# Which engine regroups q and k in front of the DMA transposes: VectorE or GpSimd

## The chip, the cores and the metric

The kernel runs on one core of a Trainium2 chip. The metric is the device time of one execution in microseconds (us); a shorter time is better. A core has engines with an instruction stream each: TensorE (PE in the profile; PEld is its weight loads), VectorE (DVE), ScalarE (ACT), GpSimd (POOL) and SyncE (SP). DMA transfers are issued from a queue of one of these engines; in this kernel from GpSimd's and SyncE's.

## The reference

Attention with a squared ReLU in place of the softmax, over 8 batches of 12 heads, 448 positions and 64 elements a head, and then a gated feed-forward layer over all 3584 tokens:

```python
scores = scale * np.matmul(q, k.transpose(0, 1, 3, 2))
attn = np.maximum(scores, 0.0) ** 2 / S
attn_out = np.matmul(attn, v)
x = attn_out.transpose(0, 2, 1, 3).reshape(B * S, H * D)      # 3584 x 768
gate = np.maximum(x @ w_gate, 0.0)                            # 768 x 1536
val = x @ w_val
return gate * val @ w_out                                     # 1536 x 768
```

Inputs and output are float32.

## The kernel before

The kernel works in 48 slots, one for each batch b (0 to 7) and each pair of heads hp (0 to 5). In a slot TensorE makes the scores of the pair (tile `sc_ps`), ScalarE takes their ReLU (`relu_part`, line 179), VectorE squares it from SBUF into SBUF (`square_part`, line 183, output `attn`), and TensorE multiplies by v (`av`, tile `xT_ps`), which VectorE copies out (line 213). The feed-forward layer of batch b-1 is cut into units and fed into the slots of batch b by `gap()`: `gv_unit` makes a gate product `g_ps` and a value product `v_ps`, of which ScalarE (line 236) and VectorE (line 241, output `hT`) make one operand of the last product; `out_unit` makes that last product (`o_ps`), and sends the rows out through SyncE's queue (line 265). `g_ps`, `v_ps` and `o_ps` share two PSUM buffers, so that a `v_ps` can begin only when the `v_ps` before it has been read by line 241.

The scores need q and k with the head's 64 elements on the partitions, that is transposed. Batches 0 and 1 are transposed on TensorE (`transposes`, line 172, copied out by VectorE in line 174). Batches 2 to 7 take another way, `dma_transposes(b)`, which is called once for each of them, in slot hp = 2 of the batch before: k (tile `kn`) is regrouped into `kr` by one copy of 128 partitions x 3072 bf16 elements (line 140), and four DMA transposes on SyncE's queue (line 143) take `kr` to `kT`; the same follows for q (`qn`, `qr`, `qT`). There is one `kr` and one `qr`, two each of `kn`, `qn`, `kT`, `qT` and v's tiles (`vn`, `vp`). In slot hp = 4 `key_pads` copies the last 64 keys out of `kT` (line 149, VectorE).

All loads are issued from GpSimd's queue (`dma_in`, line 91). `load_qk(b + 1)` and `load_v(b + 1)` stand in slot hp = 0 of batch b. Each instruction is kept in program order on its own engine (`pin`), and engines wait for one another only for data and for free buffers, so GpSimd's queue runs ahead of the others: it stops where a buffer isn't free. `load_v(b + 1)` overwrites the v tiles of batch b - 1, and so waits for the last `av` of batch b - 1. `load_qk(b + 2)`, which is next in that queue, overwrites the `kn` and `qn` of batch b, whose regrouping took place in batch b - 1, and so finds its buffers free as soon as its turn comes.

Of the kernel before, what the change touches and what calls it, by code (L numbers as in the profile page):

```python
# [16 lines left out]
def kernel(  # L17
# [14 lines left out]
    nc = tc.nc  # L32
# [25 lines left out]
    def pin(ins):  # L58
        return tc.keep_in_program_order(ins)
# [75 lines left out]
    def dma_transposes(b):  # L135

        n = b % NB
        for nat, grp, tr in ((kn_b[n], kr, kT_b[n]), (qn_b[n], qr, qT_b[n])):
            o = grp.rearrange("p i (h d) -> p i h d", d=D)
            pin(nc.vector.tensor_copy(o, nat.rearrange("p h i d -> p i h d")))  # L140
            for i in range(4):
                r = 128 if i < 3 else 64
                pin(nc.sync.dma_start_transpose(out=tr[:, :, i * 128:i * 128 + r], in_=grp[0:r, i, :]))  # L143
# [167 lines left out]
    for n, (b, hp) in enumerate(slots):  # L311
# [6 lines left out]
        if b == 0:  # L318
            relu2(*todo[0])
            if hp < HP - 1:  # L320
                kq_next = operands(b, hp + 1)
            relu2(*todo[1])
            relu2(*todo[2])
            scores_last(kq, attn)
            if prev:
                av(*prev)
            prev = this
            if hp == HP - 1:
                av(*prev)
        else:  # L330
            relu2(*todo[0])
            relu2(*todo[1])
            late.append(todo[2])
            gap()
            scores_last(kq, attn)
            if n + 1 < len(slots):
                kq_next = operands(*slots[n + 1])
            gap()
            av(*this)
            if b + 1 >= PE_B and b + 1 < B:  # L340
                if hp == 2:
                    dma_transposes(b + 1)
                if hp == 4:
                    key_pads(b + 1)
            if b > 1:
                gap()
# [46 lines left out]
```

## Time and profile before

| what | value |
|---|---|
| median of 3 runs | 446.57 us (446.33 to 449.02) |
| the profiled execution | 449.76 us, with a span of 447.7 us from the first to the last instruction |
| TensorE (PE) busy | 426.9 us, 95% of the span |
| VectorE (DVE) busy | 215.2 us, 48% |
| ScalarE (ACT) busy | 220.2 us, 49% |
| GpSimd (POOL) busy | 61.5 us, 14%, nearly all of it the issue of DMAs |
| line 140, both copies | 12 instructions, 11.4 us of VectorE |
| TensorE clock granted | 0.994 on average |

The profiled execution is one run with its own time: 2.06 us of it lie outside the span, and it is 3.2 us above the median of the three runs. Busy times are sums over an engine. TensorE has 20.8 us without work in the whole span, 8 us of them in the first 15 us. Where the batches begin on TensorE, by the first scores made from `kT` and `qT`: batch 2 at 90.5 us, batch 3 at 145.5 us, batch 6 at 297.5 us.

### The profile page before, as it was taken

What the parts mean: (1) busy time and instruction counts of PE and PEld (TensorE: products, weight loads), DVE (VectorE), ACT (ScalarE), POOL (GpSimd) and SP (SyncE); (2) the same over time, 40 slices, a digit from 0 to 9 for tenths busy, and PEclk for the clock granted to TensorE, in tenths of its full rate; (3) what the DMA queues carried; (4) which work ended last, traced back from release to release, by engine and by line L of the source; (5) the groups of instructions that cost most, each with busy time, mean ns of one, the idle gap of its engine ahead of it and who ended that gap; (6) DMA issues with size and microseconds to landing.
All of it is one profiled execution on the core that took longest, in us unless ns stands there. A gap on an engine that the chain in (4) does not pass through costs nothing.

```text
span 447.7 us, 10641 instructions
## 1 busy us (share of the span) xinstructions
PE 426.9 (95%) x4608; PEld 251.4 (56%) x4608; DVE 215.2 (48%) x382; ACT 220.2 (49%) x345; POOL 61.5 (14%) x89
## 2 busy tenths in 40 slices
PE   3879998899999999999999999999999999999995
PEld 1337554545566555665566555565556655666663
DVE  4682566535643556444653457455644445422210
ACT  3572565546454654654464565464455456442221
POOL 9624410430003100050001300020000000000000
PEclk9999999989999999999999999999999999999999
DMA  7999999997443914398153932471042200030014
GB/s 83 181 204 191 202 205 178 151 243 99 45 115 77 204 16 98 63 147 110 39 87 91 191 50 63 98 111 24 19 108 72 72 2 0 5 90 15 1 37 107
DMA packets 91887, 43.55 MB, mean 97 GB/s; under 512 B 66753, under 2 KB 88257, under 8 KB 91841
## 3 DMA queue, kind: packets, MB, share of 16 engines
q0 software_dynamic: 53568, 23.60, 42.6%
q1 hardware_dynamic: 38272, 19.28, 20.1%
q8 instruction: 36, 0.59, 0.5%
q14 instruction: 11, 0.08, 0.1%
HBM read 47.19 MB, written 11.01 MB: 130 GB/s over the span
## 4 chain that ended last, share of the span: by engine, by line
PE 79%; DMA 15%; POOL 2%; SPq 1%; DVE 1%; issue 1%; ACT 0%; POOLq 0%; DVEq 0%
PE g_ps L62 22%; PE o_ps L62 22%; PE v_ps L62 21%; PE sc_ps L62 7%; PE xT_ps L62 6%; DMA qn<-in_q_dram 5%; DMA kn<-in_k_dram 4%; DMA wv<-in_moe_w_val_dram 2%; DMA qT<-qr 2%; DMA vn<-in_v_dram 2%; SPq L143 1%; DVE attn L183 1%; POOL qn L91 1%; POOL wg L91 1%; POOL kn L91 1%
## 5 line engine op out<-in xcount | busy, mean ns | idle before, releaser
L179 ACT ACTIVATE r_sb<-sc_ps 128x896 bf16<-128x896 f32 x192 | 149.5, 826 | 43.7 <-PE sc_ps L62 43.7
L183 DVE TENSOR_TENSOR attn<-r_sb 128x896 bf16<-128x896 bf16 x192 | 104.8, 564 | 75.3 <-ACT r_sb L179 75.3
L62 PE MATMUL g_ps<-xT,wg 128*64 128x448 bf16 x1152 | 126.9, 356 | 0.2 <-DVE xT L213 0.2
L62 PE MATMUL v_ps<-xT,wv 128*64 128x448 bf16 x1152 | 125.7, 354 | 0.0
L62 PE MATMUL o_ps<-wo,hT 128*64 128x384 bf16 x1344 | 117.2, 327 | 0.0
L241 DVE TENSOR_TENSOR hT<-v_ps,g_sb 128x448 bf16<-128x448 f32 x96 | 60.0, 625 | 104.7 <-PE v_ps L62 104.7
L236 ACT ACTIVATE g_sb<-g_ps 128x448 bf16<-128x448 f32 x96 | 52.3, 545 | 106.8 <-PE g_ps L62 106.8
L62 PEld LDWEIGHTS <-hT 128*64 128x64 bf16 x1344 | 74.8, 110 | 38.1 <-issue 5.6
L62 PEld LDWEIGHTS <-wg 128*64 128x64 bf16 x1152 | 63.9, 110 | 48.9 <-issue 11.2
L62 PEld LDWEIGHTS <-wv 128*64 128x64 bf16 x1152 | 66.6, 110 | 43.3 <-issue 1.0
L262 ACT ACTIVATE o_sb<-o_ps 128x384 f32<-128x384 f32 x56 | 27.8, 496 | 72.1 <-PE o_ps L62 72.1
L213 DVE CAST xT<-xT_ps 128x448 bf16<-128x448 f32 x48 | 29.9, 624 | 23.6 <-PE xT_ps L62 22.0
L62 PE MATMUL xT_ps<-attn,vn 128*64 128x448 bf16 x288 | 37.3, 362 | 2.6 <-DVE attn L183 1.6
L91 POOL DMA_DIRECT2D vn<-in_v_dram x16 | 12.1, 765 | 191.0 <-PE xT_ps L62 186.0
L62 PE MATMUL sc_ps<-qT,kT 64*128 64x448 bf16 x216 | 26.7, 352 | 2.8 <-DMA qT<-qr 2.8
L62 PEld LDWEIGHTS <-vn 128*64 128x64 bf16 x288 | 17.0, 112 | 14.0 <-issue 3.8
L62 PE MATMUL sc_ps<-kq_sb 64*128 64x448 bf16 (+1 forms) x96 | 16.1, 417 | 2.3 <-DVE kq_sb L174 1.3
L62 PEld LDWEIGHTS <-kT 64*128 64x128 bf16 x216 | 7.6, 94 | 18.3 <-issue 15.0
L62 PE MATMUL xT_ps<-attn,vp 128*64 128x448 bf16 x96 | 17.7, 362 | 0.0
L91 POOL DMA_DIRECT2D kn<-in_k_dram x20 | 14.8, 768 | 13.6 <-PE kq_ps L172 12.7
L91 POOL DMA_DIRECT2D qn<-in_q_dram x20 | 14.7, 760 | 7.4 <-DMA qn<-in_q_dram 3.9
L91 POOL DMA_DIRECT2D vp<-in_v_dram x16 | 10.8, 692 | 17.1 <-PE g_ps L62 5.3
(27 smaller groups left out, 85.8 us busy)
## 6 DMA issues: line engine op xcount, KB each, us to landing
out_dram<-o_sb SPq DMA_DIRECT2D x56, 192.0 KB, 2.7
vn<-in_v_dram POOLq DMA_DIRECT2D x16, 288.0 KB, 7.2
kn<-in_k_dram POOLq DMA_DIRECT2D x7, 384.0 KB, 9.2
qn<-in_q_dram POOLq DMA_DIRECT2D x7, 384.0 KB, 11.2
wo<-in_moe_w_out_dram POOLq DMA_DIRECT2D x2, 1152.0 KB, 17.7
kn<-in_k_dram POOLq DMA_DIRECT2D x7, 288.0 KB, 10.0
qn<-in_q_dram POOLq DMA_DIRECT2D x7, 288.0 KB, 12.4
wg<-in_moe_w_gate_dram POOLq DMA_DIRECT2D x4, 384.0 KB, 9.5
```

Of the source, the lines that this page charges most:

```text
L62: pin(nc.tensor.matmul(o, lhsT=l, rhs=r, start=start, stop=stop, skip_group_check=True))
L91: pin(nc.gpsimd.dma_start(out=o, in_=i))
L143: pin(nc.sync.dma_start_transpose(out=tr[:, :, i * 128:i * 128 + r], in_=grp[0:r, i, :]))
L179: pin(nc.scalar.activation(r, src, AF.Relu))
L183: pin(nc.vector.tensor_tensor(dst, r, r, ALU.mult))
L213: pin(nc.vector.tensor_copy(xT[:, hp, :], ps))
L236: pin(nc.scalar.activation(g_sb, g_ps, AF.Relu))
L241: pin(nc.vector.tensor_tensor(hT[:, mf, col:col + S], v_ps, g_sb, ALU.mult))
L262: pin(nc.scalar.activation(out=o_sb[:, m], in_=o_ps, func=AF.Copy, scale=float(out_scale)))
```

## The change

The two regrouping copies of `dma_transposes` are issued on GpSimd instead of VectorE. Their operands, the DMA transposes behind them and every other line are the same. Since GpSimd's queue also holds the loads, the copies for batch b + 1 now stand in it behind `load_v(b + 1)` and ahead of `load_qk(b + 2)`.

```diff
         for nat, grp, tr in ((kn_b[n], kr, kT_b[n]), (qn_b[n], qr, qT_b[n])):
             o = grp.rearrange("p i (h d) -> p i h d", d=D)
-            pin(nc.vector.tensor_copy(o, nat.rearrange("p h i d -> p i h d")))
+            pin(nc.gpsimd.tensor_copy(o, nat.rearrange("p h i d -> p i h d")))
             for i in range(4):
                 r = 128 if i < 3 else 64
                 pin(nc.sync.dma_start_transpose(out=tr[:, :, i * 128:i * 128 + r], in_=grp[0:r, i, :]))
```

## The prediction

> **What bounds the kernel now.** I read the page's busy times and chain first, then the timelines of VectorE and TensorE around the copies, then GpSimd's own.
>
> ```profile
> PE 426.9 (95%) x4608; PEld 251.4 (56%) x4608; DVE 215.2 (48%) x382; ACT 220.2 (49%) x345; POOL 61.5 (14%) x89
> ...
> PE 79%; DMA 15%; POOL 2%; SPq 1%; DVE 1%; issue 1%; ACT 0%; POOLq 0%; DVEq 0%
> ```
>
> TensorE bounds it. Taking work off VectorE, which is half idle, brings nothing by itself. A copy counts only where TensorE waits, and the list of waits has two such places: 2.8 us for `qT` (once) and 1.6 us for squares (four times).
>
> ```profile
> 68.85 0.96 DVE L140 COPY kr<-kn 128x3072 bf16<-128x3072 bf16 x1 [0.43 <-DMA kn<-in_k_dram]
> ...
> 72.39 0.96 DVE L140 COPY qr<-qn 128x3072 bf16<-128x3072 bf16 x1 [2.58 <-DMA qn<-in_q_dram]
> ...
> 73.27 1.99 DVE L183 TENSOR_TENSOR attn<-r_sb 128x896 bf16<-128x896 bf16 x4
> ...
> 73.94 0.38 PE L62 MATMUL xT_ps<-attn,vn 128*64 128x448 bf16 x2 [0.86 <-DVE attn L183]
> ...
> 90.51 0.74 PE L62 MATMUL sc_ps<-qT,kT 64*128 64x448 bf16 x6 [2.83 <-DMA qT<-qr]
> ...
> 91.19 2.45 PE L62 MATMUL g_ps<-xT,wg 128*64 128x448 bf16 x12
> ...
> 93.43 1.89 PE L62 MATMUL v_ps<-xT,wv 128*64 128x448 bf16 x12
> ```
>
> (Timelines: start, length, engine; in brackets the idle time before and its releaser.) Both places belong to the first pair of copies, for batch 2. VectorE sits 2.58 us in front of a copy whose q hasn't landed, four squares queue behind it, and TensorE loses 0.86 us, and 0.15 and 0.16 behind that: 1.2 us. Then it waits 2.83 us for `qT`, and the next products run at a granted clock of 0.57 (91 to 95 us, by the windows): 2.45 and 1.89 us instead of 1.30 each, 1.7 us lost. The other five pairs cost TensorE nothing: the second, at 116.21 and 117.08, sits between a cast and a product of line 241 that was due at about 117.7, and no wait of TensorE follows.
>
> **What the change removes.** 12 copies of 0.95 us, 11.4 us of VectorE; on TensorE at most the 1.2 us, and these lie ahead of the wait for `qT`, which would take them back if `qT` lands when it does.
>
> **What it adds: the copy on GpSimd.** The trace has no such copy. Lowest: VectorE's own 0.95 us. Highest: GpSimd's only elementwise row with an input, the 128x128 affine_select, 349 ns; less the 100 ns of its one-element memsets that is 1.95 ns an element, so 3072 x 1.95 + 100 = 6.1 us. Between them lies ScalarE's ReLU, 896 elements in 826 ns: 3072 x 826 / 896 = 2.83 us. A copy does less for each element than a select with its comparison, and I know no reason for VectorE's rate on an engine of another kind: I take 2.83 us, and call it D. The Trainium skill (GPSIMD Engine Reference, 3.1 Elementwise) gives 1.03 cycles an element at 1.2 GHz for simple bodies, an estimate of 2.64 us; by it the sum below would be some 1.5 us less.
>
> **What moves.** Once GpSimd's queue holds the copies, they no longer stand in slot hp = 2 but run as soon as the queue reaches them, at the batch's start:
>
> ```profile
> 143.21 1.33 POOL L91 DMA_DIRECT2D vp<-in_v_dram  x2
> 144.51 1.54 POOL L91 DMA_DIRECT2D kn<-in_k_dram  x2
> ...
> 195.84 1.55 POOL L91 DMA_DIRECT2D kn<-in_k_dram  x2
> ```
>
> In place of these `kn` issues come the copies, at 144.5, 195.8, 247.2 and 298.6 us; their data landed 40 us before. Behind them on GpSimd wait only the loads of the batch after next, 2 x 2.83 = 5.7 us late: issued by about 153 and needed by the next copy at 195.8, with 10 to 13 us to landing. No cost; it would cost from about 30 us. The 48 transposes stay on SyncE behind the same output DMAs, and now run at the start of the batch instead of slot 2, beside loads; outputs come next at 185, so they hold up nobody, and `kT` is needed at the next batch's start. DMAs are the same in number and size. The third batch's pair runs when `kn` and `qn` land, at about 91.7 and 94.6 us (issues at 80.30 and 81.77, landing after 11.4 and 12.8).
>
> **Whether VectorE can run beside it.** No row has a VectorE instruction beside a GpSimd instruction that reads SBUF. Bounds: no delay, or every square waits for the copy's end. For no delay speaks that the square at 146.90 takes its usual 0.63 us beside an issue of GpSimd; but an issue reads no tile. For a delay speaks that VectorE's rates go with where its operands lie (copy from SBUF 3.2 elements a ns, square 1.6, cast from PSUM 0.7), so access to SBUF is what it spends its time on, and the copies now add another reader. I take the full wait. The Trainium skill (SBUF — State Buffer, Who interferes with whom) speaks against this change outright: a VectorE instruction with two SBUF inputs and a GpSimd instruction that reads SBUF share a port, and whichever comes second waits for the whole of the first; no trace here shows it yet. By that rule the squares wait and the products of line 241, with one input in PSUM, wait only behind them; without it the sum is that of the first rival.
>
> **The price at the start of a batch.** In the timeline before:
>
> ```profile
> 146.90 0.63 DVE L183 TENSOR_TENSOR attn<-r_sb 128x896 bf16<-128x896 bf16 x1 [4.58 <-ACT r_sb L179]
> ...
> 147.71 0.63 DVE L183 TENSOR_TENSOR attn<-r_sb 128x896 bf16<-128x896 bf16 x1 [0.18 <-ACT r_sb L179]
> ...
> 148.69 0.62 DVE L241 TENSOR_TENSOR hT<-v_ps,g_sb 128x448 bf16<-128x448 f32 x1 [0.36 <-PE v_ps L62]
> ...
> 149.23 0.92 DVE L183 TENSOR_TENSOR attn<-r_sb 128x896 bf16<-128x896 bf16 x2
> ...
> 149.75 1.30 PE L62 MATMUL v_ps<-xT,wv 128*64 128x448 bf16 x12
> ```
>
> If copy and square alternate: first copy from 144.51 to 144.51 + D, a square (0.55), second copy D, another square (0.45 to the next start), and only then line 241, due at 148.69. It is 2D + 1.0 - 4.18 = 2.5 us late; 0.44 us of slack remain before the `v_ps` at 149.75, so TensorE stands 2.0 us. If two squares slip in between the copies, line 241 is on time, and the squares of 149.23 end 2.0 us late, of which `av` at 150.88 absorbs about 1.1: 0.9 us. Middle 1.5. The batches at 195.84 and 298.6 reach their first square only 0.4 us behind the copy (196.28), and line 241 at 198.08: 2D + 1.0 - 2.24 - 0.44 = 4.0 us, or 2.7 by the other order; middle 3.4. The pair for batch 3 (from 91.7) by the same reckoning 0.7 to 2.1, say 1.0. A stand of 2.83 us was followed by the 1.7 us of low clock above; of the two longer ones I count one.
>
> The first pair: `kr` is ready 1.9 us later (D - 0.95). By the windows the DMA engines move loads at about 190 GB/s until 74 us, and the first `kT` transposes land only after 6.6 us, so part of this is hidden; `qT` lands at 90.4 plus 0 to 1.9 us. TensorE's 1.2 us are given back here by the wait. I take +1.0.
>
> Sum: 1.0 + 1.0 + 2 x 1.5 + 2 x 3.4 + 1.7 = 13.5 us on the span of 447.7, so 461.2; with the 2.06 around it 463.3, against 449.76. The runs' median is 3.2 us below the profiled one: 446.57 + 13.5 = 460.
>
> **Rivals.** (1) No delay of VectorE: the copies lie beside it, and only the first pair counts, 0 to 1.9 us: 447 to 448; at D = 6.1 it would be up to 5 us, 452. For it: nothing in the rows shows the opposite. Against: only the argument on SBUF access. (2) The wait holds and the copy is long. Each of the four starts grows by 2 us for each us of D in the alternating order: from D = 2.83 to 6.1 this adds 4 x 6.5 = 26 us, with low clock at all four (5 us more), the pair for batch 3 and the first another 10: 460 + 41 = about 500. For it: the affine_select row; against: the simpler work. (3) Faster. VectorE is no longer held 2.58 us by the q that hasn't landed, and the transposes, issued 1.9 us later, fall behind the backlog of loads and meet no competition, so that `qT` lands before TensorE, 1.2 us earlier, asks for it at 86.5: then 1.2 + 2.83 + 1.7 = 5.7 us go, 440.9. It decides only if `qT` lands 4 us earlier than now; against it stands that the next loads of `kn` and `qn`, issued at 79.41 to 82.5, share the DMA engines with the last `qT` transpose (issued 81.95, landed 8.4 us later), and would meet it later still.
>
> **How the numbers follow.** Forecast 0.50; rival 1 0.32 (0.05 of it slower by over 1%, with a long copy); rival 2 0.13; rival 3 0.05. One per cent, 4.5 us, is about what a measurement of this kernel tells from no change. Faster 0.05, same 0.27, slower 0.50 + 0.05 + 0.13 = 0.68. The range goes from 446 (rival 1's lower end with a little spread) to 480, which the full wait gives at D of about 4.2 (8 x 1.4 = 11 from the four starts, the clock 5, the other pairs 4); left out are most of rival 2 and rival 3. For the forecast alone it is 452 to 472.
>
> **What would show it.** The copies at POOL line 140 at the batch's start, of 2.8 us; squares of line 183 beside them of 2 to 3 us or with a gap in front of them; a wait of `v_ps` or `xT_ps` on VectorE of 1 to 4 us at 150, 200, 251 and 303 us; transposes about 20 us earlier. If squares beside the copies stay at 0.56 to 0.63 us without gaps, the forecast is wrong and rival 1 holds; a copy over 4.5 us makes rival 2.

## The result, and the profile after

The changed kernel takes 467.38 us (median of 6 runs, 466.45 to 468.75) against 447.28 us for the kernel before on the same chips: the ratio is 1.043, with a 95% interval of 1.039 to 1.047. The profiled execution took 466.93 us, with a span of 465.0 us, 17.3 us more than the span of before. That the medians lie 20.1 us apart comes mostly from the profiled execution of before, which was 2.5 us slower than its median; what these 2.5 us are, one profile can't show.

From the page after, the busy times, and from its list of waits (engine and line, what it waited for, us in total, times, longest) the rows that have grown on TensorE:

```profile
PE 426.1 (92%) x4608; PEld 253.7 (55%) x4608; DVE 223.5 (48%) x370; ACT 220.2 (47%) x345; POOL 94.0 (20%) x101
```
```profile
PE v_ps L62 <- DVE hT L241: 10.6, 4, 3.6
PE sc_ps L62 <- DMA qT<-qr: 10.5, 1, 10.5
```

TensorE does the same work as before (426.1 against 426.9 us) and stands longer. VectorE lost 12 copies and is busy for longer all the same, 223.5 against 215.2 us: its squares now include waiting (124.1 us in all, 104.8 before). The timeline at the start of a batch shows what the 10.6 us are. Before:

```profile
196.28 0.62 DVE L183 TENSOR_TENSOR attn<-r_sb 128x896 bf16<-128x896 bf16 x1 [2.63 <-ACT r_sb L179]
...
198.08 0.63 DVE L241 TENSOR_TENSOR hT<-v_ps,g_sb 128x448 bf16<-128x448 f32 x1 [0.37 <-PE v_ps L62]
```

After:

```profile
202.27 2.80 POOL L140 COPY kr<-kn 128x3072 bf16<-128x3072 bf16 x1
202.70 6.06 DVE L183 TENSOR_TENSOR attn<-r_sb 128x896 bf16<-128x896 bf16 x2 [2.63 <-ACT r_sb L179]
...
204.95 2.79 POOL L140 COPY qr<-qn 128x3072 bf16<-128x3072 bf16 x1
...
208.69 0.61 DVE L241 TENSOR_TENSOR hT<-v_ps,g_sb 128x448 bf16<-128x448 f32 x1
...
209.36 1.33 PE L62 MATMUL v_ps<-xT,wv 128*64 128x448 bf16 x12 [3.64 <-DVE hT L241]
```

The two squares that took about 1.4 us take 6.06. The first of them lasts 5.53 us by itself, until 0.48 us after the second copy has ended, and so waited for both copies. Line 241, which began 1.8 us behind the first square before (198.08 against 196.28), begins 6.0 us behind it, and TensorE stands 3.64 us in front of `v_ps`. The other three starts read alike, with 1.69, 1.69 and 3.63 us.

The other loss lies at the start of batch 2. Before:

```profile
77.10 6.16 SPq L143 DMA_TRANSPOSE qT<-qr  x4
...
79.41 1.63 POOL L91 DMA_DIRECT2D kn<-in_k_dram  x2 [12.68 <-PE kq_ps L172]
```

After:

```profile
71.51 5.91 SPq L143 DMA_TRANSPOSE kT<-kr  x4
...
76.42 0.75 POOL L91 DMA_DIRECT2D kn<-in_k_dram  x1 [1.39 <-PE kq_ps L172]
77.46 10.25 SPq L143 DMA_TRANSPOSE qT<-qr  x4
...
78.41 1.50 POOL L91 DMA_DIRECT2D qn<-in_q_dram  x2
...
95.15 1.30 PE L62 MATMUL sc_ps<-qT,kT 64*128 64x448 bf16 x6 [10.46 <-DMA qT<-qr]
```

The issue of the four `qT` transposes takes 10.25 us instead of 6.16, and `qT` lands at 95.1 instead of 90.4 us, although TensorE is ready for it 3.0 us earlier than before (84.7 against 87.7; 1.9 of these were there by 31 us, ahead of any copy, and belong to the two executions, not to the change). From the start of batch 2 to the end it is 369.8 us against 357.2: of these 12.6 us, 10.6 are the four waits, and most of the rest is a granted clock of 0.67 over the 5 us behind the last of them. With the 4.6 us that batch 2 starts later this makes the 17.3.

### The profile page after: what moved, and what is told of

Its sections match the earlier page's. It is cut to its first block, busy times and chain, and to the rows that moved or that the text cites. A ratio compares the mean times of both kernels' runs of the same rounds, so it can differ in the third digit from the quotient of the medians.

```text
span 465.0 us, 10638 instructions
## 1 busy us (share of the span) xinstructions
PE 426.1 (92%) x4608; PEld 253.7 (55%) x4608; DVE 223.5 (48%) x370; ACT 220.2 (47%) x345; POOL 94.0 (20%) x101
## 4 chain that ended last, share of the span: by engine, by line
PE 72%; DMA 14%; issue 3%; SPq 3%; POOL 3%; DVE 3%; ACT 1%; POOLq 0%; ACTq 0%
PE o_ps L62 21%; PE v_ps L62 20%; PE g_ps L62 19%; PE sc_ps L62 6%; PE xT_ps L62 6%; DMA vn<-in_v_dram 5%; DMA kn<-in_k_dram 5%; SPq L143 3%; DMA wg<-in_moe_w_gate_dram 2%; DVE attn L183 2%; DMA qT<-qr 2%; ACT r_sb L179 1%; POOL kn L91 1%; POOL kr L140 1%; POOL qn L91 1%
## 5 line engine op out<-in xcount | busy, mean ns | idle before, releaser
L183 DVE TENSOR_TENSOR attn<-r_sb 128x896 bf16<-128x896 bf16 x192 | 124.1, 667 | 81.1 <-ACT r_sb L179 81.0
L62 PE MATMUL v_ps<-xT,wv 128*64 128x448 bf16 x1152 | 126.5, 355 | 10.6 <-DVE hT L241 10.6
L62 PEld LDWEIGHTS <-wv 128*64 128x64 bf16 x1152 | 68.0, 111 | 53.4 <-issue 11.8
L62 PE MATMUL sc_ps<-qT,kT 64*128 64x448 bf16 x216 | 27.2, 358 | 10.5 <-DMA qT<-qr 10.5
L140 POOL COPY qr<-qn 128x3072 bf16<-128x3072 bf16 x6 | 16.7, 2780 | 5.6 <-DMA qT<-qr 4.8
L140 POOL COPY kr<-kn 128x3072 bf16<-128x3072 bf16 x6 | 16.7, 2788 | 2.5 <-DMA kn<-in_k_dram 2.5
L62 PE MATMUL sc_ps<-kq_sb 64*128 64x448 bf16 (+1 forms) x96 | 15.0, 392 | 2.3 <-DVE kq_sb L174 1.3
```

Of the source, the lines that this page charges most:

```text
L62: pin(nc.tensor.matmul(o, lhsT=l, rhs=r, start=start, stop=stop, skip_group_check=True))
L140: pin(nc.gpsimd.tensor_copy(o, nat.rearrange("p h i d -> p i h d")))
L183: pin(nc.vector.tensor_tensor(dst, r, r, ALU.mult))
```

## The experiments

Two theories had to be told apart. The first has two parts: squares of VectorE wait while GpSimd copies, and the `qT` of batch 2 is stuck behind loads that have come ahead of it. The second is that a copy moved to GpSimd brings a lasting cost of its own or by the transposes and loads that move with it.

**Memsets beside the kernel before** (`e2_memset_beside`). GpSimd writes, but reads nothing.

```diff
             pin(nc.vector.tensor_copy(o, nat.rearrange("p h i d -> p i h d")))
+            for i in range(4):
+                pin(nc.gpsimd.memset(sb[i % 2], float(i)))          # sb: two tiles of 128x768
```

> The kernel before with VectorE's own copies, and beside them eight GpSimd memsets of 128x768 bf16 for each of the six batches, into two scratch tiles, in the queue place that the copies have in the changed kernel (they feed nothing). Theory (what holds VectorE's squares is GpSimd READING SBUF): the squares beside the memsets keep 0.61 to 0.63 us, TensorE has no wait for line 241, and the time is that of before, 447 us within 2. Rival (any GpSimd instruction that touches SBUF holds the squares): squares that start while a memset runs take longer by what is left of the memsets, and TensorE waits for line 241 at the four batch starts as in the changed kernel, 1.7 and 3.6 us or in proportion to the length of the memsets.

Measured: 452.51 us, ratio 1.012 (1.007 to 1.017). There is no wait for line 241, and squares beside the memsets keep their time:

```profile
199.40 5.55 POOL L143 MEMSET sb<- 128x768 bf16 x8
```
```profile
199.84 0.63 DVE L186 TENSOR_TENSOR attn<-r_sb 128x896 bf16<-128x896 bf16 x1 [2.63 <-ACT r_sb L182]
200.65 0.62 DVE L186 TENSOR_TENSOR attn<-r_sb 128x896 bf16<-128x896 bf16 x1 [0.18 <-ACT r_sb L182]
```

That part of the theory holds. The time was 5.5 us over the 447 expected (between the two profiled executions it is 3.6), and the profile has the reason in one place, the first pair, where the memsets meet VectorE's own regrouping:

```profile
68.73 4.30 DVE L141 COPY kr<-kn 128x3072 bf16<-128x3072 bf16 x1 [2.09 <-DMA kn<-in_k_dram]
```

The copy of 0.95 us took 4.30, until 0.8 us after the last memset (66.70 + 5.51 = 72.2). TensorE then waited 3.2 us for squares, and 4.3 instead of 2.8 for `qT`. So GpSimd's writes held VectorE's copy from SBUF to SBUF in the one place where the two met, but none of its squares.

**The copies cut into four** (`e3_split`).

```diff
-            pin(nc.gpsimd.tensor_copy(o, nat.rearrange("p h i d -> p i h d")))
+            for i in range(4):
+                pin(nc.gpsimd.tensor_copy(o[:, i], nat[:, :, i, :]))
```

> The changed kernel with each copy cut into four of 128x768 (one for each i), so four short GpSimd copies after one another in place of one of 2.8 us. In the changed kernel the first square of a batch lasted until both copies were done (5.53 us at 202.70), although two instructions stood on GpSimd. Theory A (GpSimd keeps SBUF to itself as long as its instructions follow without a gap): no relief, squares of up to 5.5 us, four waits of 1.7 to 3.6 us for line 241, 467 us within 2. Theory B (held for one instruction at a time, and VectorE gets in between): a square waits at most some 0.8 us, the four waits together fall from 10.6 us to under 2, 457 us within 3.

Measured: 472.62 us, ratio 1.058 (1.054 to 1.061). No relief: one square lasts 5.50 us across seven short copies, and the four waits sum to 13.0 us.

```profile
203.03 6.66 DVE L184 TENSOR_TENSOR attn<-r_sb 128x896 bf16<-128x896 bf16 x2 [2.63 <-ACT r_sb L180]
```

The waits grew with the copies: eight pieces of 0.77 us from start to start take 0.7 us longer than two whole copies, at four starts. Theory A is much nearer than theory B, but it holds neither to the end nor in the time. The square ended 0.5 us after the seventh piece, and the eighth took 1.24 us instead of some 0.85: there VectorE did get in between two pieces. And the time is 5.6 us over the 467 expected. Of these 2.4 are the longer waits; the wait for `qT` is 2.5 us shorter. The rest goes with the clock, 0.974 on average against 0.984: the 12 products behind each of the four waits took 1.77 to 2.45 us, where in the changed kernel they took 1.33 behind three of the four.

**load_v first for batch 3** (`e4_v_first`), on the changed kernel.

```diff
+            if b == 2:
+                load_v(b + 1)
             load_qk(b + 1)
-            load_v(b + 1)
+            if b != 2:
+                load_v(b + 1)
```

> The changed kernel; for batch 3 alone load_v stands ahead of load_qk in GpSimd's queue, so that k and q of batch 3 load only after the last av of batch 1, behind the DMA transposes of batch 2. In the changed kernel those loads were issued at 76.4 to 79.9 us, ahead of the four qT transposes (77.5 to 87.7), and TensorE waited 10.5 us for qT, against 2.8 before. Theory (the transposes share the DMA engines with loads that are ahead of them): qT lands at about 86 to 87, the wait falls to 1 to 3 us, the time by 7 to 10, to 458 us. Rival (qT is late because the GpSimd copies make kr and qr later): the wait stays over 8 us, and the time within 2 us of 467.

Measured: 458.72 us, ratio 1.027 (1.023 to 1.030). The wait for `qT` falls from 10.5 to 0.2 us with the copies still on GpSimd:

```profile
84.30 0.74 PE L62 MATMUL sc_ps<-qT,kT 64*128 64x448 bf16 x6 [0.15 <-DMA qT<-qr]
```

The waits for line 241 stay (11.8 us, five of them). From issue to landing a `qT` transpose takes 2.6 us by the median, 10.9 in the changed kernel. So it was the loads ahead of the transposes, not the copies, that made `qT` late; what in the DMA engines lets them hold the transposes up isn't shown.

**The copies held to the end of slot 2** (`e7_placed`), on the changed kernel.

```diff
                 if hp == 2:
+                    if b > 1:
+                        pin(nc.gpsimd.tensor_copy(mark, xT_of[b][:, hp, 0:1]))   # mark: 128x1
                     dma_transposes(b + 1)
```

> The changed kernel; from batch 3's pair on a GpSimd copy of one element of xT ahead of the regrouping copies makes them wait for the end of slot hp = 2, where VectorE had them and where the next squares are 3 to 5 us away in the timeline of before. Theory (the loss is the overlap of copies and squares): copies of the same 2.8 us; the pairs for batches 3, 5 and 7 (at 116, 219, 322 us of before) meet no square, those for 4 and 6 (169, 272) hold two squares and cost TensorE some 1.3 us each; the waits for line 241 fall from 10.6 to about 2.6 us, 457 us within 3, and the wait for qT at batch 2 stays. Rival (the loss comes from moving the copies to GpSimd at all, wherever they stand: a lasting cost of each, or of the transposes and loads behind them): the time stays within 3 us of 467.

Measured: 457.02 us, ratio 1.021 (1.017 to 1.026). The copies take 2.75 to 3.14 us, and the waits for line 241 are

```profile
PE v_ps L62 <- DVE hT L242: 2.7, 2, 1.3
```

two of 1.3 us, at the two batches where squares stand near. The same copies in another place cost TensorE a quarter of the waiting.

**Copies that feed nothing** (`e1_copy_beside`), for batches 3 to 7 beside the kernel before; the regrouping, its transposes and the loads of batch 2 stay as they were.

```diff
             pin(nc.vector.tensor_copy(o, nat.rearrange("p h i d -> p i h d")))
+            for i in range(4 if b > PE_B else 0):
+                pin(nc.gpsimd.tensor_copy(sb[i % 2], wg_sb[2].rearrange("p k f -> p (k f)")[:, 768 * i:768 * i + 768]))
```

> The kernel before, whose regrouping stays on VectorE, with eight GpSimd copies of 128x768 bf16 from weights into two scratch tiles for each of the batches 3 to 7 (they feed nothing; none for batch 2), in the queue place of the changed kernel's copies. Split copies held the squares as long as whole ones. Theory (GpSimd's reads beside the squares are the loss, not the move of the regrouping, of its transposes or of the loads): four waits for line 241 of some 2 to 4 us, 13 us together as with the split copies, 1 to 2 us at batch 2's start, so 461 us within 3. Rival (the loss comes with the moved transposes and loads): these stay where they were, and the time is 447 us within 2.

Measured: 457.09 us (four runs, 454.04 to 461.14), ratio without the slowest of them 1.019 (1.014 to 1.025). The loss is there without any move, though smaller than expected. At three starts the square waited for the end of all pieces, as here at 148 us; at two it got in between them:

```profile
148.15 4.86 DVE L186 TENSOR_TENSOR attn<-r_sb 128x896 bf16<-128x896 bf16 x2 [4.58 <-ACT r_sb L182]
```
```profile
201.84 2.09 DVE L186 TENSOR_TENSOR attn<-r_sb 128x896 bf16<-128x896 bf16 x2 [2.63 <-ACT r_sb L182]
```

At these two GpSimd was held in its turn: its eight pieces took 7.62 us, where they took 6.22 at the other three. What decides between the two stays open. These pieces write two scratch tiles in turn, which those of the split kernel don't; but they do so at all five starts.

**The first pair alone on GpSimd** (`e5_first_alone`).

```diff
+            eng = nc.gpsimd if b == PE_B else nc.vector
-            pin(nc.gpsimd.tensor_copy(o, nat.rearrange("p h i d -> p i h d")))
+            pin(eng.tensor_copy(o, nat.rearrange("p h i d -> p i h d")))
```

> The changed kernel with GpSimd copies for batch 2 alone; batches 3 to 7 are regrouped by VectorE as before. Theory (the two losses are separate: qT of batch 2, and the squares at the later batch starts): no wait for line 241, a wait of 8 to 11 us for qT with low clock behind it, 452 us within 3. Rival (the first pair costs what was predicted, 1 us, and qT came late in the changed kernel by chance or by the later copies): 447 to 449 us.

Measured: 452.59 us, ratio 1.011 (1.008 to 1.014). The wait for `qT` is 5.7 us, less than expected, since TensorE itself came 1.7 us later: four squares stood on VectorE behind the copy out of a `kT` that landed only at 83.4 us (80.6 in the changed kernel). The time is as expected. So the first pair alone costs about 5 us, five times what was predicted for it.

**q alone on GpSimd** (`e10_q_alone`): half of the copies.

```diff
+            eng = nc.gpsimd if grp is qr else nc.vector
-            pin(nc.vector.tensor_copy(o, nat.rearrange("p h i d -> p i h d")))
+            pin(eng.tensor_copy(o, nat.rearrange("p h i d -> p i h d")))
```

> The kernel before with q's copies alone on GpSimd, k's on VectorE: one copy of 2.8 us at a batch's start instead of two. Theory (a square waits for the end of the copies, and line 241 has slack): where the copy starts 2.4 us ahead of the first square nothing is lost, where it starts 0.4 us ahead line 241 is 1.5 us late and TensorE stands 1.1 us: 2 us in all from the four starts, against 10.6 with both copies, and 0 to 3 us at batch 2 for qT: 451 us within 2. Rival (the loss goes by the copies' time): half of the loss of the changed kernel, 457 us.

Measured: 453.95 us, ratio 1.014 (1.011 to 1.018). The waits for line 241 are two, 1.9 us together, as worked out: half the copies give less than a fifth of the 10.6 us. The sum was 1 us over its range, because batch 2 cost more again: a wait of 5.8 us for `qT`, and in front of it 1.7 us for squares that stood behind a `kT` landing at 83.3 us.

**Both remedies on the changed kernel** (`e8_placed_v_first`: the mark and `load_v` first).

> Both remedies together on the changed kernel: the later pairs held to the end of slot hp = 2, and load_v ahead of load_qk for batch 3. Each alone took 8.7 and 10.4 us off 467.4. Theory (the two losses are all there is): they add, 448 us within 2, no faster than before. Rival (they overlap, or a third cost of a GpSimd copy is left): 451 us or more.

Measured: 445.69 us, ratio 0.9960 (0.9935 to 0.9985): with all copies on GpSimd, 0.4% faster than the kernel before, and 2.3 us under the 448 expected. No third cost shows. Of the loss, the two waits of 1.3 us for line 241 are left; shorter waits at the first pair make up for them (1.0 us for `qT` and 1.0 for squares, against 2.8 and 1.6 in the kernel before).

**load_v first on the kernel before** (`e6_before_v_first`).

> The kernel before (copies on VectorE) with load_v ahead of load_qk for batch 3 alone. Theory (the last qT transposes shared the DMA engines with the loads issued at 79.4 to 82.5 us): the wait of 2.8 us for qT and the 1.7 us of low clock behind it go, 442 to 444 us. Rival (qT takes 8 us to land for a reason of its own, the loads of v and of batch 2 ahead of it): 446 to 447 us.

Measured: 446.02 us, ratio 0.9962 (0.9944 to 0.9980), a gain of 0.4% where 0.8 to 1.2% was expected. The wait for `qT` is gone, but TensorE stands in another place:

```profile
74.19 0.38 PE L62 MATMUL xT_ps<-attn,vn 128*64 128x448 bf16 x2 [3.28 <-DVE attn L183]
...
77.35 3.23 PE L62 MATMUL o_ps<-wo,hT 128*64 128x384 bf16 x24
```

VectorE stands behind the copy of a q that hasn't landed, four squares stand behind VectorE, and `o_ps` after that runs at 3.23 instead of 2.14 us. What the prediction read as 1.2 us in one execution is 3.6 in this one: TensorE came 2.2 us earlier to a q that landed no earlier (the copy of q began at 72.64 us, at 72.39 before).

**The first pair on GpSimd, load_v first** (`e9_first_v_first`), the other pairs on VectorE.

> GpSimd copies for batch 2 alone, VectorE's for batches 3 to 7, and load_v ahead of load_qk for batch 3: what the runs so far point to. Theory: VectorE no longer stands behind a copy whose q hasn't landed (1.2 us in the profile of before, 3.6 in that of the kernel before with load_v first), qT lands in time, and no square of a later batch is held (2.7 us in the run with both remedies): 442.5 to 444.5 us, faster than before and than the two kernels at 446. Rival (at 446 something else bounds the first 90 us, such as the landing of the loads): 445 to 447 us.

Measured: 442.20 us (441.49 to 442.78), ratio 0.988 (0.985 to 0.991), faster than the kernel before and than the changed one. It is the one pair that was seen to gain by the move: GpSimd can wait for the landing q without holding up squares meanwhile, if the loads behind are kept from overtaking.

## Why the prediction was right, and where it was wrong

The forecast was 460 us, the measurement 467.4: slower, as forecast, inside the range to 480, and 13.5 us forecast against about 20. That it still lies inside is in part luck: the range above 460 was worked out from a longer copy, and what made the difference was another term.

- The length of the copy: 2.83 us taken from ScalarE's rate, 2.79 measured. No row tied the one engine's rate to the other's, so that it came so near is luck. The Trainium skill (GPSIMD Engine Reference, 3.1 Elementwise) with its 1.03 cycles gave an estimate of 2.64; the trace lies 6% above it.
- The full wait of the squares: right, and shown by moving the copies, by copies that feed nothing, and by memsets that hold no square. The Trainium skill (SBUF — State Buffer, Who interferes with whom) says that a VectorE instruction with two SBUF inputs contends with a GpSimd instruction that reads SBUF and not with one that only writes, and that VectorE's copies in a 2-port mode contend with both; the 5.53 us, the 0.63 us and the 4.30 us agree, though no run shows the mode of that copy. It speaks of a wait for the whole of one instruction; here a square waited for two, and in the split kernel for seven.
- The four starts: 9.8 us in the sum as the middle of two orders, 10.6 measured. Neither order was it: the first square waited for both copies. For line 241 that comes to nearly what the alternating order gave (2.0 and 4.0, measured 1.7 and 3.6), since the same two copies and two squares stand ahead of it.
- Low clock after one of the two long stands, 1.7 us: after the one at 317 us the clock is 0.67 for 5 us, after the one at 209 it stays 1.00. Right, if by a guess.
- The pair for batch 3, 1.0 us: no TensorE wait. It came apart, since the second copy had to wait for the `qT` transposes to free `qr`.
- The failing term is the first pair: +1.0 us predicted, 4.6 in the spans (against a profiled execution of before that was 2.5 us slow) and about 5 by the run with it alone. The step was "`qT` lands at 90.4 plus 0 to 1.9 us", which moved the transposes and left the loads in their place. But the loads moved. `load_qk` for batch 3 overwrites the `kn` and `qn` of batch 1, which TensorE itself transposes, so that TensorE releases these loads; and VectorE, freed of the copy that waits for q, let TensorE come earlier. The loads were issued from 76.4 instead of 79.4 us, ahead of transposes issued from 77.5 instead of 77.1. Of these 3.0 us the two executions brought 1.9 along and the change 1.1. But the lead of 1.9 survives only without the wait on VectorE: in `e1_copy_beside`, up to batch 2 the kernel before and as early (62.1 us at the transposes in front, 62.2 in the changed kernel), TensorE stood 2.4 us for squares behind the copy of q, and the loads went out at 78.7, after transposes issued from 76.3.
- The third rival had named the sharing with these loads, in its objection ("would meet it later still"), and the sum didn't count it. Of the rival itself, half holds. That transposes issued later meet no competition was wrong. That the waits at this pair can go was right, but it takes a second edit that holds the loads back: then it is 442.2 us.

With the first pair 3.6 us over its term, the pair for batch 3 1.0 under and the four starts 0.8 over, the sum of 13.5 becomes 16.9, against 17.3 in the spans.

Rival 1, no wait of VectorE, is out; rival 2 needed a long copy, and the copy is short.

## What to carry to other kernels

Before a copy is moved to GpSimd, look at which VectorE instructions will stand beside it and what waits behind them: what counted was not the 2.8 us of a copy but whether squares fell into it, and the same copies cost 10.6 us at the start of a batch and 2.7 us two slots later. A queue that runs ahead of the others runs a moved instruction where the queue is, not where the program text has it. And when a wait is taken away ahead of a release, ask what the release lets go earlier and what that will overtake.

## What the runs showed of the hardware that was not expected

Cutting GpSimd's work into short instructions gave VectorE hardly a way in: with copies of 0.77 us from start to start a square stood 5.50 us across seven of them and got in only ahead of the eighth. With copies that feed nothing it got in early at two starts of five, and why is open. GpSimd memsets, which slowed no square, held VectorE's copy between SBUF tiles for the rest of their row of eight (4.30 us instead of 0.95, seen once).
